# A six-layer cross network on one core: part of the transposes of input and output moved from TensorE to transposing DMAs

**Chip, cores, metric.** One Trainium2 chip (trn2), one NeuronCore. The metric is device time in microseconds (us), the median of the executions of a kernel; all executions told of here are of the fast state, none more than 1.5% above the fastest of its kernel. A span, read from a profile, runs from the first to the last instruction of one execution and is some 1.8 us shorter than that execution's time.

## The reference

```python
B, F, D, L = 1024, 26, 32, 6
Din = 832                      # min(F*D, 1024): six chunks of 128 columns and a ragged one of 64
# x0: (1024, 832), ws: (6, 832, 832), bs: (6, 832), all bfloat16
def reference(x0, ws, bs):
    x = x0
    for l in range(6):
        x = x0 * (x @ ws[l] + bs[l]) + x
    return x
```

## The kernel before

The layers work on the transposed activations: features on the partitions, the 1024 rows of the batch in the free dimension. So x0 has to be turned once at the start, and the result once at the end. Both are done on TensorE by matmuls against an identity, with an eviction from PSUM by ScalarE or VectorE in turn.

```python
# loads, all issued by SyncE in this order (shortened)
add_dma("sp", bs_nat[:, :], bs[:, :], ...)
for h in range(2):                      # x0 in two halves of 512 rows, 832 KB each
    add_dma("sp", xnat[:, h*4:(h+1)*4, :], x0[h*512:(h+1)*512, :], ...)
add_w_tail(0)                           # the last 64 rows of ws[0], twice
for dc in range(7):                     # ws[0] by columns of 128, 192 KB each
    add_dma("sp", w_sb[:, 0, 0:6, dc*128:...], ws[0, 0:768, dc*128:...], ...)
    if dc == 1:
        plan.op("sp", lambda e: None, reads=[("xnat", ...all...)], record=False)  # wait for x0
# ... ws[1] to ws[5], whole ...

# TensorE: 40 warm-up matmuls on the identity, the biases, then
for h in range(2):
    for kc in range(6):                 # 4 transposes into one PSUM bank, one eviction
        for i2 in range(4):
            pe_mm(bank, ..., xnat[:, bt, kc*P:(kc+1)*P], ident, ...)
        evac_copy(consumer, x0T[:, kc, hcols(h)], ps[bank], ...)
# ... the ragged chunk ("fold"): two halves of the batch packed on 128 partitions ...

# each layer: 3 groups of 2 chunks x 2 halves (28 matmuls of 128x512 each), then a fold group (14)
# per job: ScalarE adds the bias out of PSUM into tbuf, VectorE multiplies by x0T, then adds x
for l in range(6):
    pending_T = []
    for gi, dcs in enumerate(dc_groups):
        emit_group(l, dcs)
        if last:                        # output transposes one group late, and a store per pair
            if pending_T:
                emit_out_transposes(pending_T.pop(0))
            pending_T.append(dcs)
    emit_fold_group(l, 0)
    # last layer: the rest of the pending transposes, then those of the fold and its store
```

## Time and profile before

| | before |
|---|---|
| time, median of 5 (later of 15) | 138.91 us |
| span of the profiled execution (its own time: 139.71 us) | 137.9 us |
| layer 0 begins on TensorE | 10.43 us |
| group 2 of the last layer done | 125.6 us |
| last eviction done | 133.1 us |

The program is a chain of three stretches, and a gain in one is read from that stretch: up to layer 0 (loads and input transposes), from there to the end of the last layer's group 2 (TensorE alone), and from there to the end (VectorE, then a store). The prediction below shows the lines. In them PE is TensorE, PEld its weight loads, ACT ScalarE, DVE VectorE, POOL GpSimd, and SPq SyncE's queue of DMA issues; `out<-in` are the tiles written and read, xN is how many instructions a line takes together, and `[0.19 <-ACT tbuf L488]` says that the engine stood idle for 0.19 us, until that instruction released it.

### The profile page before, as it was taken

How to read it: one execution, taken by the hardware profiler on the slowest of the kernel's cores; microseconds unless marked ns; L12 is line 12 of the kernel's file. 1: busy time of each engine (PE TensorE's matmuls, PEld its weight loads, DVE VectorE, ACT ScalarE, POOL GpSimd, SP SyncE). 2: the span in 40 equal slices, each digit the busy share in tenths (PEclk: the TensorE clock that was granted, in tenths of full speed). 3: DMA queues.
4: the chain of work that ended last, by engine and by line, in shares of the span. 5: the costliest groups of instructions: out<-in, count | busy, mean ns of one | idle time of the engine just before them, and what ended most of it. 6: DMA issues, size and time to landing. Idle time of an engine off the chain costs nothing.

```text
span 137.9 us, 1914 instructions
## 1 busy us (share of the span) xinstructions
PE 127.1 (92%) x748; PEld 57.2 (41%) x748; DVE 68.7 (50%) x169; ACT 60.7 (44%) x104; POOL 0.7 (1%) x6
## 2 busy tenths in 40 slices
PE   5969999999999999999999999999999999899600
PEld 5954343444334343434343443434343434345300
DVE  0072174574538290926553562917274726573950
ACT  4274336091706361542725172806336442725920
POOL 2000000000000000000000000000000000000000
PEclk9999999999999999999999999999999999999995
DMA  2998999999700000000000000000000000005075
GB/s 49 400 235 188 257 331 363 357 322 321 277 3 0 0 2 7 0 0 0 0 0 0 0 5 0 0 0 0 0 0 5 0 0 0 0 0 152 0 217 130
DMA packets 15604, 12.48 MB, mean 90 GB/s; under 512 B 6886, under 2 KB 15596, under 8 KB 15596
## 3 DMA queue, kind: packets, MB, share of 16 engines
q1 hardware_dynamic: 15596, 12.37, 29.7%
q8 instruction: 6, 0.10, 0.3%
q14 instruction: 2, 0.02, 0.0%
HBM read 10.66 MB, written 1.70 MB: 90 GB/s over the span
## 4 chain that ended last, share of the span: by engine, by line
PE 83%; DMA 5%; DVE 4%; ACT 2%; issue 1%; SPq 1%; DVEq 0%; ACTq 0%
PE ps L339 83%; DMA xnat<-in_x_dram 5%; ACT tbuf L488 2%; DVE xT L524 2%; DVE ybuf L509 1%; DVE xnat L359 1%; SPq L266 1%; DVEq L182 0%; ACTq L137 0%
## 5 line engine op out<-in xcount | busy, mean ns | idle before, releaser
L339 PE MATMUL ps<-xT,w_sb 128*128 128x512 bf16 (+3 forms) x490 | 96.9, 381 | 0.4 <-ACT tbuf L488 0.4
L488 ACT ACTIVATE tbuf<-ps,bias_sb 128x512 bf16<-128x512 f32 (+1 forms) x84 | 51.2, 687 | 65.5 <-PE ps L339 65.4
L339 PEld LDWEIGHTS ps<-xT,w_sb 128*128 128x128 bf16 (+3 forms) x490 | 39.3, 99 | 57.1 <-issue 15.1
L509 DVE TENSOR_TENSOR ybuf<-tbuf,x0T 128x512 bf16<-128x512 bf16 x78 | 32.8, 420 | 54.3 <-ACT tbuf L488 54.3
L524 DVE TENSOR_TENSOR xT<-ybuf,xT 128x512 bf16<-128x512 bf16 x65 | 27.6, 425 | 2.2
L339 PE MATMUL ps<-x0T,w_sb 128*128 128x512 bf16 (+3 forms) x98 | 19.3, 380 | 0.0
L339 PEld LDWEIGHTS ps<-x0T,w_sb 128*128 128x128 bf16 (+3 forms) x98 | 7.8, 99 | 11.3 <-issue 3.0
L359 DVE CAST x0T<-ps 128x512 bf16<-128x512 f32 x6 | 3.8, 684 | 7.4 <-PE ps L339 7.4
L524 DVE TENSOR_TENSOR xT<-ybuf,x0T 128x512 bf16<-128x512 bf16 x13 | 5.5, 425 | 0.4
L339 PE MATMUL ps<-ident 128*128 128x128 bf16 x40 | 4.1, 298 | 1.5 <-POOL ident L234 1.5
L339 PE MATMUL ps<-ident,xT 128*128 128x128 bf16 (+1 forms) x56 | 3.7, 216 | 1.7 <-DVE xT L524 0.9
L354 ACT ACTIVATE x0T<-ps 128x512 bf16<-128x512 f32 (+1 forms) x8 | 4.2, 596 | 0.9 <-PE ps L339 0.8
L339 PEld LDWEIGHTS ps<-ident 128*128 128x128 bf16 x40 | 3.9, 142 | 1.5 <-POOL ident L234 1.5
L339 PE MATMUL ps<-ident,xnat 128*128 128x128 bf16 (+1 forms) x56 | 3.4, 220 | 1.2 <-DMA xnat<-in_x_dram 1.2
L339 PEld LDWEIGHTS ps<-ident,xT 128*128 128x128 bf16 (+1 forms) x56 | 2.9, 97 | 3.1 <-DVE xT L524 1.1
L359 DVE CAST xnat<-ps 128x512 bf16<-128x512 f32 (+1 forms) x7 | 4.2, 643 | 0.0
L354 ACT ACTIVATE xnat<-ps 128x512 bf16<-128x512 f32 (+1 forms) x7 | 3.7, 578 | 0.6 <-PE ps L339 0.6
L339 PEld LDWEIGHTS ps<-ident,xnat 128*128 128x128 bf16 (+1 forms) x56 | 2.9, 99 | 1.5 <-DMA xnat<-in_x_dram 1.4
L410 ACT ACTIVATE bias_sb<-ps 128x36 f32<-128x36 f32 x1 | 0.2, 201 | 3.8 <-PE ps L339 3.8
L376 ACT ACT_TABLE_LOAD x1 | 1.3, 1283 | 0.7 <-PEq L774 0.7
L339 PE MATMUL ps<-ident,bs_nat 6*128 6x6 bf16 (+1 forms) x8 | 0.4, 169 | 0.0
L422 ACT ACTIVATE bias_sb<-ps 64x6 f32<-64x6 f32 x2 | 0.3, 172 | 0.1
(8 smaller groups left out, 1.4 us busy)
## 6 DMA issues: line engine op xcount, KB each, us to landing
w_sb<-in_ws_dram SPq DMA_DIRECT2D x5, 1248.0 KB, 11.7
xnat<-in_x_dram SPq DMA_DIRECT2D x2, 832.0 KB, 5.8
out_dram<-xnat SPq DMA_DIRECT2D x3, 512.0 KB, 3.7
w_sb<-in_ws_dram SPq DMA_DIRECT2D x12, 104.0 KB, 9.4
w_sb<-in_ws_dram SPq DMA_DIRECT2D x6, 192.0 KB, 4.9
out_dram<-xnat SPq DMA_DIRECT2D x1, 128.0 KB, 4.2
w_sb<-in_ws_dram SPq DMA_DIRECT2D x1, 96.0 KB, 3.7
bs_nat<-in_bs_dram SPq DMA_DIRECT2D x1, 9.8 KB
```

The lines of the kernel that those rows point to most:

```text
L266: return e.dma_start(out=out_ap, in_=in_ap).then_inc(sem, 16)
L339: return e.matmul(out_ap, lhsT=lhsT, rhs=rhs, start=start, stop=stop, tile_position=tile_position,)
L354: return e.activation(out=out_ap, in_=in_ap, func=ACTF.Copy)
L359: return e.tensor_copy(out=out_ap, in_=in_ap)
L376: lambda e: e.activation(out=act_scratch[:, :], in_=ident[:, 0:8], func=ACTF.Copy),
L410: lambda e: e.activation(out=bias_sb[:, 0:NKF, :], in_=ps[bank_][:, 0 : NKF * L], func=ACTF.Copy,),
L422: return lambda e: e.activation(out=bias_sb[hf * HP : hf * HP + R, F, :], in_=ps[bank][hf * HP : hf * HP + R, F * L : (F + 1) * L], func=A ...
L488: return e.activation(out=tbuf[p0:p1, tslot, :], in_=ps[bank][p0:p1, :], func=ACTF.Identity, bias=bias_sb[p0:p1, kc_slot, l : l + 1], scal ...
L509: return e.tensor_tensor(out=ybuf[p0:p1, yb, :], in0=tbuf[p0:p1, tslot, :], in1=x0_ap, op=ALU.mult,)
L524: return e.tensor_tensor(out=xout_ap, in0=ybuf[p0:p1, yb, :], in1=xin_ap, op=ALU.add,)
```

## The change

Its intent is to let the DMA engines, which are idle in the last layers, do part of the transposing. At the front, chunks 4 and 5 of x0 (`NPE = 4` stay on TensorE) come transposed straight from DRAM; at the end, chunks 0 to 3 of the result are transposed from SBUF to SBUF and stored in pairs. The loads are regrouped, SyncE's wait for x0 is dropped, and chunks 4, 5 and the ragged tail are stored as one.

```diff
+        NPE = 4
         for h in range(NH):
             add_dma("sp",
-                xnat[:, h * BT_PER_H : (h + 1) * BT_PER_H, :],
+                xnat[:, h * BT_PER_H : (h + 1) * BT_PER_H, 0 : NPE * P],
 ...
+        add_dma("sp", xnat[:, :, DF : DF + R], x0[:, DF : DF + R]...)      # ragged tail, 128 KB
 ...
             if l == 0:
-                add_w_tail(0)
                 for dc in range(NKC):
                     add_dma("sp", w_sb[:, 0, 0:NKF, c0 : c0 + cw], ...)
                     if dc == min(1, NKC - 1):
-                        plan.op("sp", lambda e: None, reads=[("xnat", ...)], record=False)
+                        for kc in range(NPE, NKF):
+                            add_dma_t("sp", x0T[:, kc, :], x0[:, kc * P : (kc + 1) * P], ...)
+                        add_w_tail(0)
 ...
-            for kc in range(NKF):
+                for kc in range(NPE):                                      # 40 transposes, not 56
 ...
+        def emit_out_dma_transposes(dcs):
+            for c in dcs:
+                plan.dma("sp", lambda e: e.dma_start_transpose(
+                    out=xnat[:, :, c * P : (c + 1) * P], in_=xfin[:, c, :]), ...)
+            emit_out_dma(dcs[0] * P, (dcs[-1] + 1) * P, list(dcs))
 ...
+            # last layer: all groups, DMA transposes of groups 0 and 1, the fold group,
+            # then TensorE's transposes of chunks 4, 5 and the fold, and one store of 640 KB
+                emit_out_dma(c0, D, list(tail_dcs) + ([F] if FOLD else []))
```

More of the change, by code (lines that the diff above doesn't have):

```diff
@@ L177, in bass_standalone__dcn_v2_cross__recsys_kernel @@
     NWARM = 40
+    DMA_T_OUT = True
+    DMA_T_IN = True
     NY = 2
@@ L270, in bass_standalone__dcn_v2_cross__recsys_kernel, with add_dma_t, emit @@
         add_dma("sp", bs_nat[:, :], bs[:, :], writes=[("bs_nat",)])
+        def add_dma_t(q, out_ap, in_ap, writes, reads=()):
+            sem = new_dma_sem()
+            def emit(e, out_ap=out_ap, in_ap=in_ap, sem=sem):
+                return e.dma_start_transpose(out=out_ap, in_=in_ap).then_inc(sem, 16)
+            plan.dma(q, emit, done=(sem, 16), reads=reads, writes=writes)
+        NPE = 4
         for h in range(NH):
-            bts = range(h * BT_PER_H, (h + 1) * BT_PER_H)
             add_dma(
                 "sp",
-                xnat[:, h * BT_PER_H : (h + 1) * BT_PER_H, :],
-                x0[h * NCOL : (h + 1) * NCOL, :].rearrange("(bt p) d -> p bt d", p=P),
-                writes=[("xnat", bt, kc) for bt in bts for kc in range(NKC)],
-            )
+                xnat[:, h * BT_PER_H : (h + 1) * BT_PER_H, 0 : NPE * P],
+                x0[h * NCOL : (h + 1) * NCOL, 0 : NPE * P].rearrange("(bt p) d -> p bt d", p=P),
+                writes=[("xnat", bt, kc) for bt in range(h * BT_PER_H, (h + 1) * BT_PER_H) for kc in range(NPE)],
+            )
+        add_dma(
+            "sp",
+            xnat[:, :, DF : DF + R],
+            x0[:, DF : DF + R].rearrange("(bt p) d -> p bt d", p=P),
+            writes=[("xnat", bt, F) for bt in range(BT)],
+        )
         def wkey(l, kc, dc, hf):
@@ L310, in bass_standalone__dcn_v2_cross__recsys_kernel @@
                     if dc == min(1, NKC - 1):
-                        plan.op(
+                        for kc in range(NPE, NKF):
+                            add_dma_t(
+                                "sp",
+                                x0T[:, kc, :],
+                                x0[:, kc * P : (kc + 1) * P],
+                                writes=[("x0T", kc, h2) for h2 in range(NH)],
+                            )
+                        add_w_tail(0)
+                        if False: plan.op(
                             "sp",
@@ L317, in bass_standalone__dcn_v2_cross__recsys_kernel @@
                                 for kc in range(NKC)
-                            ],
+                            ]
+                            + [("x0T", kc, h) for kc in range(NKF) for h in range(NH)],
                             record=False,
@@ L431, in bass_standalone__dcn_v2_cross__recsys_kernel @@
         for h in range(NH):
-            for kc in range(NKF):
-                bank = next_bank()
-                for i2 in range(BT_PER_H):
-                    bt = h * BT_PER_H + i2
-                    pe_mm(
-                        bank,
-                        ps[bank][:, i2 * P : (i2 + 1) * P],
-                        xnat[:, bt, kc * P : (kc + 1) * P],
-                        ident[:, :],
-                        True,
-                        True,
-                        reads=[("xnat", bt, kc), ("ident",)],
-                    )
-                consumer = "act" if cnt % 2 == 0 else "dve"
-                cnt += 1
-                evac_copy(
-                    consumer,
-                    x0T[:, kc, hcols(h)],
-                    ps[bank][:, :],
-                    bank,
-                    writes=[("x0T", kc, h)],
-                )
+            if True:
+                for kc in range(NPE):
+                    bank = next_bank()
+                    for i2 in range(BT_PER_H):
+                        bt = h * BT_PER_H + i2
+                        pe_mm(
+                            bank,
+                            ps[bank][:, i2 * P : (i2 + 1) * P],
+                            xnat[:, bt, kc * P : (kc + 1) * P],
+                            ident[:, :],
+                            True,
+                            True,
+                            reads=[("xnat", bt, kc), ("ident",)],
+                        )
+                    consumer = "act" if cnt % 2 == 0 else "dve"
+                    cnt += 1
+                    evac_copy(
+                        consumer,
+                        x0T[:, kc, hcols(h)],
+                        ps[bank][:, :],
+                        bank,
+                        writes=[("x0T", kc, h)],
+                    )
             if FOLD and h % 2 == 1:
@@ L679, in emit_out_transposes, with emit_out_transposes_fold @@
             emit_out_dma(dcs[0] * P, (dcs[-1] + 1) * P, list(dcs))
-        def emit_out_transposes_fold():
+        def emit_out_transposes_fold(store=True):
             assert BT_PER_H * R <= NCOL
@@ L712, in emit_out_transposes_fold, with emit @@
                     )
-            emit_out_dma(DF, DF + R, [F])
+            if store:
+                emit_out_dma(DF, DF + R, [F])
+        def emit_out_dma_transposes(dcs):
+            for c in dcs:
+                sem = new_dma_sem()
+                def emit(e, c=c, sem=sem):
+                    return e.dma_start_transpose(
+                        out=xnat[:, :, c * P : (c + 1) * P], in_=xfin[:, c, :]
+                    ).then_inc(sem, 16)
+                plan.dma(
+                    "sp",
+                    emit,
+                    done=(sem, 16),
+                    reads=[xkey(L, c, h) for h in range(NH)],
+                    writes=[("xnat", bt, c) for bt in range(BT)],
+                )
+            emit_out_dma(dcs[0] * P, (dcs[-1] + 1) * P, list(dcs))
         dc_groups = [list(range(i, min(i + 2, NKF))) for i in range(0, NKF, 2)]
@@ L717, in bass_standalone__dcn_v2_cross__recsys_kernel @@
             last = l == L - 1
-            pending_T = []
-            for gi, dcs in enumerate(dc_groups):
-                emit_group(l, dcs)
-                if last:
+            if not last:
+                for dcs in dc_groups:
+                    emit_group(l, dcs)
+                if FOLD:
+                    for g in range(NG):
+                        emit_fold_group(l, g)
+                continue
+            if DMA_T_OUT:
+                n_early = len(dc_groups) - 1 if FOLD else len(dc_groups) - 1
+                for gi, dcs in enumerate(dc_groups):
+                    emit_group(l, dcs)
+                for gi in range(max(n_early, 0)):
+                    emit_out_dma_transposes(dc_groups[gi])
+                tail_dcs = dc_groups[-1] if dc_groups else []
+                if FOLD:
+                    for g in range(NG):
+                        emit_fold_group(l, g)
+                for c in tail_dcs:
+                    for h in range(NH):
+                        bank = next_bank()
+                        for i2 in range(BT_PER_H):
+                            bt = h * BT_PER_H + i2
+                            pe_mm(
+                                bank,
+                                ps[bank][:, i2 * P : (i2 + 1) * P],
+                                xfin[:, c, bt * P : (bt + 1) * P],
+                                ident[:, :],
+                                True,
+                                True,
+                                reads=[xkey(L, c, h), ("ident",)],
+                            )
+                        consumer = "act" if tcnt[0] % 2 == 0 else "dve"
+                        tcnt[0] += 1
+                        evac_copy(
+                            consumer,
+                            xnat[:, h * BT_PER_H : (h + 1) * BT_PER_H, c * P : (c + 1) * P],
+                            ps[bank][:, 0 : BT_PER_H * P].rearrange(
+                                "p (bt d) -> p bt d", d=P
+                            ),
+                            bank,
+                            writes=[
+                                ("xnat", bt, c)
+                                for bt in range(h * BT_PER_H, (h + 1) * BT_PER_H)
+                            ],
+                        )
+                if FOLD:
+                    emit_out_transposes_fold(store=False)
+                c0 = tail_dcs[0] * P if tail_dcs else DF
+                emit_out_dma(c0, D, list(tail_dcs) + ([F] if FOLD else []))
+            else:
+                pending_T = []
+                for gi, dcs in enumerate(dc_groups):
+                    emit_group(l, dcs)
@@ L724, in bass_standalone__dcn_v2_cross__recsys_kernel @@
                     pending_T.append(dcs)
-            if FOLD:
-                for g in range(NG):
-                    emit_fold_group(l, g)
-                    if last and pending_T:
-                        emit_out_transposes(pending_T.pop(0))
-            if last:
+                if FOLD:
+                    for g in range(NG):
+                        emit_fold_group(l, g)
+                        if pending_T:
+                            emit_out_transposes(pending_T.pop(0))
                 while pending_T:
```

## The prediction

> **What bounds the kernel now.** I read the page's busy times first, then the chain that ended last, then the first 12 us and the last 20 us instruction by instruction, and last the DMA rates in stretches of 1 us.
>
> ```profile
> PE 127.1 (92%) x748; PEld 57.2 (41%) x748; DVE 68.7 (50%) x169; ACT 60.7 (44%) x104; POOL 0.7 (1%) x6
> DMA  2998999999700000000000000000000000005075
> PE 83%; DMA 5%; DVE 4%; ACT 2%; issue 1%; SPq 1%; DVEq 0%; ACTq 0%
> ```
>
> The reader is to see that TensorE is the bound, and that the DMA engines are idle from slice 12 to slice 35, so the weights are no limit once the layers run. What is not TensorE lies at both ends, and the instructions in order of time show it:
>
> ```profile
> 5.91 1.51 PE L339 MATMUL ps<-ident,xnat 128*128 128x128 bf16 x24
> 8.62 1.87 PE L339 MATMUL ps<-ident,xnat 128*128 128x128 bf16 x32 [1.21 <-DMA xnat<-in_x_dram]
> 10.43 19.29 PE L339 MATMUL ps<-x0T,w_sb 128*128 128x512 bf16 x98
> 29.65 88.59 PE L339 MATMUL ps<-xT,w_sb 128*128 128x512 bf16 x448
> 118.17 1.07 PE L339 MATMUL ps<-ident,xT 128*128 128x128 bf16 x16
> 120.54 5.25 PE L339 MATMUL ps<-xT,w_sb 128*128 128x512 bf16 x25 [0.19 <-ACT tbuf L488]
> 125.71 1.07 PE L339 MATMUL ps<-ident,xT 128*128 128x128 bf16 x16
> 126.71 2.03 PE L339 MATMUL ps<-xT,w_sb 128*64 128x512 bf16 x14
> ```
>
> Layer 0 begins at 10.43 us, after x0 was loaded in two halves and turned by 56 transposes on TensorE; the second half made TensorE wait until 8.62. From 10.43 to 118.17 it never pauses: layer 1 begins 19.22 us after layer 0. In the last layer 32 of 56 output transposes stand in front of or between the layer's own matmuls. After TensorE's main work the end is a chain of VectorE work and one store:
>
> ```profile
> 125.61 0.69 ACT tbuf L488
> 129.59 0.71 DVE xnat L359 x2
> 131.59 0.60 DVE xnat L359
> 132.78 0.33 DVE xnat L359
> ```
>
> The last full group of matmuls is done at 125.6, the last eviction at 133.1; the two last stores are issued at 132.87 and 133.34, and the program ends at 137.9. In the outside time there is 1.0 us more than in the span (138.91 against 137.9); I keep that offset.
>
> **What the Trainium skill says.** (1) "DMA: Bandwidth & Descriptors", section "DMA Transpose (X-bar)": the hardware reorders on the write side, into SBUF only, for 2-byte types, issued from SP or ACT, and transposes on one queue need no wait among them. The change keeps to all of it. (2) The same page, "Latency and other measured facts": 261 GB/s was measured for one transposing kernel, and about 350 to 400 for contiguous data. A 128x1024 bf16 chunk is 262,144 bytes, so an estimate from this page is 1.0 us of transfer. (3) "VectorE: DVE Perf Modes", section "The three transpose paths", gives 1309 ns for a 128x128 bf16 block by the DMA crossbar against 390 ns on TensorE. Taken eight times over for a chunk, that would be an estimate of 10.5 us. The two pages are a factor of ten apart for our size, and the trace of before has no DMA transpose that could decide; for TensorE the trace shows far less than that page's 390 ns in a row: 16 transposes in 1.07 us, 0.067 us each. (4) "DMA: Bandwidth & Descriptors", "Queues, rings and completion order": on each engine the descriptors are consumed in ring order. So what is issued first delays what is issued after it; the trace agrees, since the first half of x0 landed 4.7 us after its issue and the second, issued 0.45 us later, 6.9 us after.
>
> **The change at the front.** x0 is loaded as two pieces of columns 0 to 511 (512 KB each), then a 128 KB ragged tail, then the weight columns 0 and 1 of layer 0, then two DMA transposes straight from DRAM (chunks 4 and 5, 256 KB each), then the weight tails and the other columns. The wait of SyncE for x0 before the third weight column is gone. TensorE does 40 transposes in place of 56.
>
> ```profile
> 3.00:4.00 1.00, 1.00 (x12) 1.00 (x11) 0.00 (x0) 0.00 (x0) 0.00 (x0) 1.00 0.86 298
> 4.00:5.00 1.00, 1.00 (x12) 1.00 (x10) 0.00 (x0) 0.00 (x0) 0.00 (x0) 1.00 1.04 401
> 8.00:9.00 1.00, 0.38 (x7) 0.38 (x8) 0.45 (x1) 0.22 (x1) 0.00 (x0) 1.00 1.30 224
> ```
>
> The last number of these stretches is GB/s. Adding up the stretches, 0.37 MB have moved by 4.0 us, then 0.4 MB per us while x0 rows of 1664 B move, and 224 GB/s when the 256 B rows of weight columns do. In before the 1.70 MB of x0 are through at about 7.4 and release TensorE at 8.6, 1.2 us later. In after 1.05 MB are through at 5.7; the 0.13 MB tail at 224 GB/s at 6.3; the two columns (0.39 MB) at 8.05, landing at about 9.2. TensorE, which can begin at 5.97 as now (its warm-up ends then), needs 16, 16 and 8 transposes, about 2.5 us, and is ready at 8.5. So layer 0 begins at about 9.2, now bound by the weight columns: 1.2 us gained.
>
> The two transposes follow. At 224 GB/s, which I take because their source rows are 256 B as well, each occupies the queue 1.17 us; they land at 10.4 and 11.6. Chunk 4 is needed after 16 matmuls of 0.2125 us (12.6), chunk 5 at 13.5. Behind them are 0.21 MB of weight tails and columns 2 and 3: through at 13.1, landing at 14.3, needed 28 matmuls (5.95 us) after the start, at 15.2. So the slack is 0.9 us for both transposes together: more than about 1.6 us each and group 1 waits for its weights, more than about 2.1 us each and group 0 waits for its chunk.
>
> **The change at the end.** Chunks 0 to 3 of the result go by four DMA transposes from SBUF to SBUF, chunk pairs stored as before; chunks 4, 5 and the tail stay on TensorE, after the fold group, in one store of 640 KB. Group 2's last matmul now comes 115.2 us after layer 0 began (125.6 - 10.43). Its own work is five layers of 19.24, then 11.6 for two groups (to 118.17, counted from 106.6) and 5.8 for the third: 113.6. The difference, 1.6 us, is 16 transposes (1.07) and the pauses for banks next to them (0.5); it goes. With the start at 9.2, group 2 ends at 122.8; call it T.
>
> From T: ScalarE's first eviction 0.7, then four VectorE pairs of about 0.82 to T+4.0 (as at 126.3 to 129.6 now). Today two evictions of 0.64 come before the fold pair; now the fold pair follows at once (T+4.85), then two evictions of 0.65 and a small one of 0.41: T+6.6, where it takes 7.5 now. Meanwhile ScalarE does its three evictions to about T+5.8. The store is issued at T+6.8 = 129.6. Now the last store lands 4.2 us after issue and has 512 KB in front of it; the 640 KB at about 340 GB/s are 1.9 us, with 0.9 before the data and 1.4 after (both as in the last store now): 4.2, and 0.2 to the end. Span 134.0, time 135.0. Sum of gains: 1.2 at the start, 1.6 inside the last layer, 0.9 in the VectorE chain, 0.2 in the store, 3.9 of 137.9.
>
> Chunks 0 and 1 are ready near T-8 and T-7 and chunks 2 and 3 near T-2.5 and T-0.8. If a transpose takes up to about 3 us from issue to landing, the second pair is in SBUF at about T+4, its store is out of the way by T+7, and nothing shows. I add 0.3 us for what I have not seen: 135.3.
>
> **The rivals.** A: as above, hidden. For it: page (2), idle DMA engines in the last layers. B: the transposes move data at a third of that, 3 to 4 us of queue each. At the end that still nearly hides; at the front it doesn't: at 3.3 us each the two take 4.3 us more than 2 times 1.17, of which 0.9 is slack, and the start's gain is gone: about 3.4 us lost, time about 138.5. The narrow place is thus the front, not the end. C: page (3) holds, 10 us each. Layer 0 then waits until about 30 us for chunk 5 (about 15 us lost), and at the end four in a row from T-8 last 42 us, some 25 us beyond the present end: 165 to 180 us. D: with SyncE's wait gone, weights crowd x0. Against it: they are behind x0 in the same ring, so at most tenths of a us.
>
> **Range and chances.** I give A about 0.5, B 0.2 with a spread from 136 to 142, C or something between B and C 0.3. A gives 134 to 136; two per cent faster is 136.1, so A is on the near side with 1 us to spare. That makes 0.5 faster, 0.2 within 2%, 0.3 slower. The range runs from A at its best, 133.6, to 150, and leaves out only the worse part of C.
>
> **What would show it.** In the profile after: layer 0's first matmul near 9.2 us, with the wait before it ended by weight columns; no pause of TensorE at chunks 4 and 5 or before group 1 (a wait on x0T by a DMA of over 0.5 us there is B or C); time from issue to landing of the transposes near 2 to 3 us; from group 2's end to the last eviction 6.6 us; no store of chunks 2 and 3 in flight when the last is issued. I am wrong if the transposes take over 2 us of queue each, or if issuing one keeps SyncE for several us.

## The result, and the profile after

The changed kernel takes 134.29 us (8 runs, 133.93 to 134.5) against 138.91 (15 runs). The ratio is 0.966, with a 95% interval of 0.9647 to 0.9674. Here and below a ratio is the mean time of one kernel's runs over that of the other's of the same rounds, so not quite the ratio of the medians quoted.

TensorE's instructions in order of time in the kernel after, at the front (start, duration, what; an idle time before stands in brackets, and there is none after the first row):

```profile
1.51 4.45 PE L363 MATMUL ps<-ident 128*128 128x128 bf16 x40 [1.51 <-POOL ident L236]
5.89 0.46 PE L363 MATMUL ps<-ident,bs_nat 6*128 6x6 bf16 x8
6.29 2.79 PE L363 MATMUL ps<-ident,xnat 128*128 128x128 bf16 x40
9.01 19.29 PE L363 MATMUL ps<-x0T,w_sb 128*128 128x512 bf16 x98
```

Layer 0 begins at 9.01 us in place of 10.43, and from its first instruction to the end of the last layer's matmuls at 124.4 TensorE no longer waits for anything: not for x0, not for the two transposed chunks, not for weights. (A start read from one trace is good to some tenths: the same 40 warm-up matmuls took 4.10 us in the trace before, 4.45 here and 3.66 in that of end_only below.) In the chain that ended last TensorE is now one piece from there:

```profile
1.51 120.97 PE ps L363 x660
122.48 0.69 ACT tbuf L513
...
128.45 0.33 DVE xnat L383
```

Group 2 of the last layer ends at 122.48, so 113.47 us after layer 0 began; the last eviction ends at 128.78, 6.3 us later; the span is 132.7. What the DMAs took, from the table of issues (count, KB, us from issue to landing), is this:

```profile
out_dram<-xnat SPq DMA_DIRECT2D x2, 512.0 KB, 3.1
out_dram<-xnat SPq DMA_DIRECT2D x1, 640.0 KB, 3.4
...
xnat<-xT SPq DMA_TRANSPOSE x4, 3.2
x0T<-in_x_dram SPq DMA_TRANSPOSE x2, 4.5
```

A transpose from SBUF to SBUF lands 3.2 us after its issue, one from DRAM at the busy front 4.5. The SyncE instructions of the end show how long issuing keeps SyncE, and that the work is done in time:

```profile
113.31 2.82 SPq L746 DMA_TRANSPOSE xnat<-xT  x2
118.07 0.39 SPq L663 DMA_DIRECT2D out_dram<-xnat  x1
119.12 2.85 SPq L746 DMA_TRANSPOSE xnat<-xT  x2
123.85 5.39 SPq L663 DMA_DIRECT2D out_dram<-xnat  x2
```

Two transposes take 2.8 us to issue, a store 0.39. The second pair is stored from 123.85 on and is out of the way 2 us before the last store is issued at 128.87.

### The profile page after: what moved, and what is told of

The parts are those of the page before. It is cut to its first block, busy times and chain, and to the rows that moved or that the text cites.

```text
span 132.7 us, 1811 instructions
## 1 busy us (share of the span) xinstructions
PE 124.7 (94%) x700; PEld 55.2 (42%) x700; DVE 65.0 (49%) x163; ACT 57.7 (44%) x98; POOL 0.7 (1%) x6
## 4 chain that ended last, share of the span: by engine, by line
PE 91%; DVE 4%; ACT 1%; issue 0%; DVEq 0%; POOLq 0%; POOL 0%
PE ps L363 91%; DVE ybuf L534 1%; DVE xT L549 1%; DVE xnat L383 1%; ACT tbuf L513 1%; DVEq L184 0%; POOLq L184 0%; POOL ident L233 0%; POOLq L236 0%; POOLq L866 0%
## 5 line engine op out<-in xcount | busy, mean ns | idle before, releaser
L383 DVE CAST x0T<-ps 128x512 bf16<-128x512 f32 x4 | 2.5, 684 | 7.4 <-PE ps L363 7.4
L378 ACT ACTIVATE x0T<-ps 128x512 bf16<-128x512 f32 (+1 forms) x6 | 3.3, 596 | 0.1
L363 PE MATMUL ps<-ident,xT 128*128 128x128 bf16 (+1 forms) x24 | 1.9, 212 | 1.4 <-DVE xT L549 1.4
L363 PE MATMUL ps<-ident,xnat 128*128 128x128 bf16 (+1 forms) x40 | 2.8, 243 | 0.0
L363 PEld LDWEIGHTS ps<-ident,xT 128*128 128x128 bf16 (+1 forms) x24 | 1.1, 96 | 2.3 <-DVE xT L549 2.3
L378 ACT ACTIVATE xnat<-ps 128x512 bf16<-128x512 f32 (+1 forms) x3 | 1.5, 524 | 0.4 <-PE ps L363 0.4
L383 DVE CAST xnat<-ps 128x512 bf16<-128x512 f32 (+1 forms) x3 | 1.6, 595 | 0.0
```

The costliest lines, as they stand in the source:

```text
L363: return e.matmul(out_ap, lhsT=lhsT, rhs=rhs, start=start, stop=stop, tile_position=tile_position,)
L378: return e.activation(out=out_ap, in_=in_ap, func=ACTF.Copy)
L383: return e.tensor_copy(out=out_ap, in_=in_ap)
```

## The experiments

Each is an edit of the kernel after or of the kernel before; ratios are against the kernel before.

### One end alone: front_only and end_only

front_only is the kernel after with `DMA_T_OUT = False` (the branch with the old end):

```diff
-    DMA_T_OUT = True
+    DMA_T_OUT = False
```

> The changed kernel with the old end (all 56 output transposes on TensorE). If the front's gain is what the two profiles show (layer 0 begins at 9.01 us in place of 10.43) and it passes undiminished to the end, 1.4 us of the 4.6 belong to it: about 137.5 us, layer 0 beginning near 9.0. A rival, that the whole gain is made at the end and an earlier front is eaten by something later, expects 138.9.

end_only is the kernel before with the last layer's code of the kernel after:

```diff
+            if DMA_T_OUT:   # the last layer of the kernel after, word for word
+                ... emit_out_dma_transposes(groups 0 and 1); one store of chunks 4, 5 and tail
```

> The old front with the changed end (four DMA transposes, merged last store). If the parts add up: 138.9 less 3.2, about 135.7 us, layer 0 beginning at 10.4, group 2's end near 123.9, last store landing about 3.4 us after its issue. If the end's gain were only there with the early front, it would be above 136.5.

front_only: 137.75 us, ratio 0.9899 (0.9864 to 0.9935), layer 0 begins at 9.02. end_only: 135.76 us, ratio 0.975 (0.9721 to 0.9778), layer 0 begins at 10.54. The product 0.9899 x 0.975 is 0.965, the changed kernel's ratio 0.966: within the noise (front_only's interval is 0.5 us to either side) the two ends are independent, with about 1.4 us (0.0101 of 138.9) at the front and 3.5 us (0.025 of 138.9) at the end. The rivals of both expectations fall.

In front_only the pauses for banks are still there, in TensorE's instructions of the last layer:

```profile
116.54 1.07 PE L363 MATMUL ps<-ident,xT 128*128 128x128 bf16 x16
117.75 0.39 PE L363 MATMUL ps<-xT,w_sb 128*128 128x512 bf16 x1
118.33 0.39 PE L363 MATMUL ps<-xT,w_sb 128*128 128x512 bf16 x1 [0.19 <-ACT tbuf L513]
118.91 5.25 PE L363 MATMUL ps<-xT,w_sb 128*128 128x512 bf16 x25 [0.19 <-ACT tbuf L513]
```

After 16 transposes (1.07 us) single matmuls wait for ScalarE's evictions; with the DMA transposes neither the transposes nor the waits are in the trace. One rival was not run: the transposes of chunks 0 to 3 left on TensorE, but placed after all of the layer's matmuls. What a new order alone would give of the 3.5 us is thus not shown.

### What of the front's gain is the DMA transpose's: pe_in and no_wait

```diff
-        NPE = 4
+        NPE = 6     # pe_in: the kernel after, all six chunks of x0 on TensorE
```

> The changed kernel, but all six chunks of x0 go by TensorE: columns 0 to 767 are loaded in two halves, no DMA transpose at the front, still no wait of SyncE. My theory, that the front gains because fewer bytes of x0 stand before TensorE's transposes and there are 16 fewer of them, expects layer 0 near 10.2 and 135.5 us. The rival, that the gain comes from the dropped wait and the new order of the loads and not from the DMA transposes, expects 134.3 us.

pe_in: 135.13 us, ratio 0.9704 (0.9675 to 0.9733); layer 0 begins at 9.78. That lies between end_only (0.975) and the kernel after (0.966), so both sides were half right: regrouping the loads without any DMA transpose gives 0.0046 of 138.9, 0.6 us, and the transposes of chunks 4 and 5 the other 0.0044, also 0.6 us. Each of these ratios has an interval of 0.2 to 0.4 us to either side, so the split is good to some tenths. TensorE's front in pe_in:

```profile
5.99 1.51 PE L363 MATMUL ps<-ident,xnat 128*128 128x128 bf16 x24
7.75 1.87 PE L363 MATMUL ps<-ident,xnat 128*128 128x128 bf16 x32 [0.25 <-DMA xnat<-in_x_dram]
9.78 2.56 PE L363 MATMUL ps<-x0T,w_sb 128*128 128x512 bf16 x11 [0.16 <-ACT x0T L378]
```

The second half of x0 releases TensorE at 7.75, where it did at 8.62 in the kernel before and at 8.51 in end_only, which has the same end as pe_in. To see whether the dropped wait is the cause, no_wait drops that alone in the kernel before:

```diff
-                    if dc == min(1, NKC - 1):
-                        plan.op("sp", lambda e: None, reads=[("xnat", bt, kc) ...], record=False)
```

> The kernel before, with only SyncE's wait for x0 dropped. pe_in has shown that 0.6 us of the front's gain needs no DMA transpose. If the wait was what cost it, layer 0 begins near 9.8 us and the time is 0.6 less, ratio about 0.995. My prediction (rival D there) said that the wait matters by tenths at most: then the ratio is 1.000 within 0.002, and the 0.6 us come from the ragged tail and the weight tails moved behind.

no_wait: 139.03 us, ratio 1.0007 (0.9995 to 1.0019). The wait is worth nothing. So, by elimination, the 0.6 us come from the rest of the regrouping: the ragged tail apart from the halves, and the weight tails moved back. At the 0.4 MB per us of the front the 0.13 MB of tail that no longer comes with the halves would be 0.33 us (an estimate). The trace of pe_in shows more: the second half landed at 7.71 and the tail at 8.30 (issued at 1.67 and 2.20), so TensorE starts on the half 0.6 us before all of x0 is there. What the moved weight tails add was not separated.

### Is the front the narrow place: dup_in and npe2

dup_in issues each front transpose twice, the second time into a scratch tile:

```diff
                             add_dma_t("sp", x0T[:, kc, :], x0[:, kc * P : (kc + 1) * P], ...)
+                            add_dma_t("sp", xdup[:, kc - NPE, :], x0[:, kc * P : (kc + 1) * P], ...)
```

> The changed kernel with each of the two front transposes issued twice, the second time into a scratch tile that nobody reads (the output stays right). That adds 2.8 us of issue and of queue ahead of the weight tails and columns. If the slack at the front is between 0.2 and 0.9 us as I worked out, TensorE pauses 1.9 to 2.6 us in layer 0 before group 1 and the time is 136.2 to 136.9. If there is slack of 3 us or more, 134.3 as without.

dup_in: 136.95 us, ratio 0.9856 (0.9812 to 0.99). That is 2.66 us over the kernel after (136.95 - 134.29), a shade above the expected band: nearly all of the 2.8 us that I had counted for the two more transposes shows. TensorE's instructions in layer 0:

```profile
8.20 4.77 PE L370 MATMUL ps<-x0T,w_sb 128*128 128x512 bf16 x20
13.87 1.04 PE L370 MATMUL ps<-x0T,w_sb 128*128 128x512 bf16 x4 [0.91 <-DMA x0T<-in_x_dram]
15.58 0.95 PE L370 MATMUL ps<-x0T,w_sb 64*128 64x512 bf16 x4 [0.67 <-DMA w_sb<-in_ws_dram]
17.08 0.60 PE L370 MATMUL ps<-x0T,w_sb 128*128 128x512 bf16 x2 [0.55 <-DMA w_sb<-in_ws_dram]
17.85 13.03 PE L370 MATMUL ps<-x0T,w_sb 128*128 128x512 bf16 x68 [0.16 <-DMA w_sb<-in_ws_dram]
```

First chunk 5 comes late, then the weight tails, then the weight columns of group 1. The instructions that write the weights, in the stretch that holds columns 2 and 3, give their landing; first the kernel after (issue from 9.9 to 10.6 us, then us from issue to landing):

```profile
L268 SPq DMA_DIRECT2D w_sb<-in_ws_dram x2: 541/566/592, 9.9 to 10.6; - x2
DMA to landing us min/median/max: 4.2/4.2/4.2
```

Column 2 was issued at 9.93 and landed at 14.2, column 3 at 10.57 and 14.8. Group 1 begins at 14.84 with two matmuls on column 2; its third is the first that reads column 3:

```profile
15.28 0.38 PE L363 MATMUL ps<-x0T,w_sb 128*128 128x512 bf16 x1
```

The slack that the prediction put at 0.9 us is thus about 0.5 for column 3 in this trace, and 0.7 for column 2. In dup_in, the same for column 3 alone:

```profile
L269 SPq DMA_DIRECT2D w_sb<-in_ws_dram x1: 540/540/540, 14.5 to 14.5; - x1
DMA to landing us min/median/max: 3.3/3.3/3.3
```

It was issued at 14.53, 4.0 us later (the last of the four transposes kept SyncE 2.25 us), but landed sooner after it, at 17.8. The matmul that reads it first begins the last row of TensorE's instructions above, at 17.85, 2.6 us later than in the kernel after: the 3.0 us by which the column landed later, less the slack of 0.5. That agrees with the 2.66 us of the times.

npe2 moves two more chunks of x0 to DMA transposes:

```diff
-        NPE = 4
+        NPE = 2
```

> The changed kernel with chunks 2 to 5 of x0 by DMA transpose in place of 4 and 5. My theory says that the front is the narrow place: SyncE issues a transpose in 1.4 us and each stays in the queue about as long, so two more of them push weight columns 2 and 3 back by 2.8 us beyond a slack of under 0.9. TensorE then waits in layer 0 for x0T and for weights, and the time is about 136.5. The rival, that transposes by DMA are cheap and more of them are better, expects layer 0 to begin near 8.3 us without a pause, and 133.7.

npe2: 136.17 us (134.77 to 136.68), ratio 0.978 (0.9722 to 0.9838), near the 136.5 expected. (By the 2% rule this one is unclear against the kernel before; against the kernel after, 0.9647 to 0.9674, the intervals don't touch.) The profiled execution was the one of 134.77, and its trace is not that of the others, which took 136.15 and more. It shows layer 0 beginning at 7.00 and then pausing twice for transposed chunks (0.38 and 0.52 us); where the other executions lose some 1.4 us more, no trace shows. Enough is measured to say that four transposes at the front are worse than two.

### The other end's limit: all_out

```diff
-                n_early = len(dc_groups) - 1 if FOLD else len(dc_groups) - 1
+                n_early = len(dc_groups)
-                tail_dcs = dc_groups[-1] if dc_groups else []
+                tail_dcs = []
```

> The changed kernel with chunks 4 and 5 of the result by DMA transpose too, stored as a pair, and the tail on its own. A transpose from SBUF takes 1.3 us to issue and 3.2 us to land; the last one is issued near 126.5 and lands at 129.7, only then is its pair stored, where TensorE's path is ready at 128.8. My theory expects about 0.8 us more than the changed kernel, 135.1. The rival, that taking the last work from TensorE and from the evictions helps here as it does for chunks 0 to 3, expects 134.0 or less.

all_out: 135.27 us, ratio 0.973 (0.9704 to 0.9756), 1.0 us above the kernel after and near the 135.1 expected. The stores of the end in its SyncE instructions:

```profile
124.51 2.85 SPq L746 DMA_TRANSPOSE xnat<-xT  x2
129.21 1.00 SPq L663 DMA_DIRECT2D out_dram<-xnat  x2
```

The last pair is ready to be stored at 129.21, although TensorE and the evictions are done at 127.8 in this trace. For work that nothing follows, the DMA's 3.2 us from issue to landing are on the path; on TensorE half a chunk takes 0.40 us for its four transposes and 0.6 to 0.7 for its eviction.

### What the last store is worth: merge_store and before_again

merge_store makes the last two stores of the kernel before into one:

```diff
+        def emit_out_transposes(dcs, store=True):
 ...
-                        emit_out_transposes(pending_T.pop(0))
+                        emit_out_transposes(pending_T.pop(0), store=False)   # the last pair
 ...
-            emit_out_dma(DF, DF + R, [F])
+            emit_out_dma(DF - 2 * P, DF + R, [F - 2, F - 1, F])
```

> The kernel before, with only its last two stores (512 KB and 128 KB) made one of 640 KB after the last eviction. My prediction put the gain of the store at 0.2 us; the profiles show 0.9 less from the last eviction to the end. If the merging makes that difference, about 138.0 us; if it was something else (the store of chunks 2 and 3 being out of the way, or chance in the one profile of before), 138.7 or more.

merge_store: 138.91 us, ratio 0.9975 (0.9946 to 1.0004). By the point value the merging is worth some 0.3 us, and nothing is not excluded. The 0.9 us by which the store's part differed between the first two profiles needed another explanation, so the kernel before was run unchanged for a second trace.

> The kernel before, unchanged, for a second trace. In the first trace the last two stores took 3.7 and 4.2 us to land, where the same stores took 3.1 and 3.4 in front_only, and its span was 137.9 where unprofiled runs had 137.1. If that was chance of one execution, this trace has stores of 3.1 to 3.4 us and a span near 137.1; if it belongs to the kernel, 3.7 to 4.2 us and 137.9 again. The time is that of before, 138.9 to 139.2.

before_again: 138.95 us, ratio 1.0005 (0.9991 to 1.0018), and a span of 137.0. Its stores:

```profile
out_dram<-xnat SPq DMA_DIRECT2D x3, 512.0 KB, 3.1
...
out_dram<-xnat SPq DMA_DIRECT2D x1, 128.0 KB, 3.4
```

In the first trace these rows read 3.7 and 4.2. Its last stores were late by chance: that execution's span of 137.9 is 0.8 above the 137.1 or so of unprofiled ones. From the last eviction to the end it is 4.1 us in the second trace and 3.8 in that of merge_store, which agrees with the 0.3 us of its ratio.

### Versions beyond the change: nwarm32, split_store, both

```diff
-    NWARM = 40
+    NWARM = 32
```

> The changed kernel with 32 warm-up matmuls in place of 40. In the trace after, TensorE never pauses from 1.51 us on: the 40 warm-up matmuls (4.45 us) now stand on the path to layer 0, while the first half of x0 has landed about 0.9 us before they end and weight column 1 about 0.4 us before layer 0 begins. My theory expects layer 0 to begin about 0.35 us earlier, held by weight column 1, and 133.9 us. If the front is held by loads as my prediction said, nothing changes: 134.3.

nwarm32: 133.74 us, ratio 0.9618 (0.9594 to 0.9642), 0.6 us below the kernel after. Its front:

```profile
1.52 3.53 PE L363 MATMUL ps<-ident 128*128 128x128 bf16 x32 [1.52 <-POOL ident L236]
...
8.52 18.98 PE L363 MATMUL ps<-x0T,w_sb 128*128 128x512 bf16 x95 [0.17 <-DMA w_sb<-in_ws_dram]
```

The warm-up was on the path after the change. With it shorter, TensorE waits in layer 0 for weight column 1 (issued at 3.86, landed at 8.48), the bound that the prediction had named.

split_store cuts the last store:

```diff
+        def emit_out_dma(c0, c1, chunk_keys, bts=None):                  # bts: rows to store
 ...
-                emit_out_dma(c0, D, list(tail_dcs) + ([F] if FOLD else []))
+                emit_out_dma(c0, DF, list(tail_dcs), range(0, BT_PER_H))     # rows of the first half
+                emit_out_dma(c0, DF, list(tail_dcs), range(BT_PER_H, BT))    # of the second
+                emit_out_dma(DF, D, [F])                                     # ragged tail
```

> The changed kernel with its last store of 640 KB cut in three: chunks 4 and 5 of the first half of the rows as soon as they are evicted (about 1.1 us before the rest), of the second half, and the ragged tail. If the end after the last eviction is set by the bytes that are left (640 KB took 1.9 us to move), 0.4 to 0.6 us are gained: 133.8. If two more issues on SyncE and the small rows of the tail eat it, 134.3.

split_store: 133.69 us, ratio 0.9613 (0.9589 to 0.9637), 0.6 us below the kernel after, as expected.

> The two together. If they are independent, as they stand at the two ends: 133.4 us, ratio to the kernel before about 0.960.

both: 133.29 us (133.03 to 134.51), ratio 0.9583 (0.9559 to 0.9608), the fastest of all and close to the sum of the two gains (134.29 less 0.55 and 0.60 is 133.1). The profiled execution was the slowest, 134.51 us, and shows why: in layer 0 TensorE stands for 1.09 us in group 1, before weight column 3.

```profile
8.88 6.00 PE L363 MATMUL ps<-x0T,w_sb 128*128 128x512 bf16 x28 [0.43 <-DMA w_sb<-in_ws_dram]
15.97 13.03 PE L363 MATMUL ps<-x0T,w_sb 128*128 128x512 bf16 x67 [1.09 <-DMA w_sb<-in_ws_dram]
```

Column 3 was issued at 10.76 and landed at 15.93, 1.2 us later than in the kernel after, while group 1 began only 0.3 us earlier (14.50 against 14.84). Why it landed late the trace does not tell, and the five faster executions (133.03 to 133.44) have no trace.

## Why the prediction was right, point by point

The time was said to be 135.3 with gains of 3.9 us in the span; it is 134.29, inside the range and faster by more than 2% as the chances leaned. The range, up to 150, was wide, so the terms say more than it does.

- **Rival A, B or C.** A holds: the transposes are hidden. A chunk's transpose keeps SyncE 1.24 to 1.44 us; from SBUF its data move for about 1.25 us at 190 to 230 GB/s, where the prediction took 224 GB/s and 1.17 us for one from DRAM. Rival C (10 us) is refuted by 3.2 and 4.5 us to landing; B (3 to 4 us of queue) by the 1.25 us, and at the front by the 1.4 us between the landings of the two (10.4 and 11.8). The prediction was right to give rival D, the dropped wait, no weight, as no_wait shows.
- **The start of layer 0.** Predicted 9.2, found 9.01. The reason given was not the one that bound, so that the number is near is in part luck: weight column 1 was to be last, at 9.2, but it landed near 8.6 (issued at 3.74, 4.9 us), while TensorE, said to be ready at 8.5, was ready only at 9.01. It never paused, and the path ran through its own warm-up, biases and 40 transposes. The column was first read by the third matmul, at 9.46, so it had 0.8 us to spare; in nwarm32, with TensorE earlier, TensorE waits for it.
- **The two chunks at the front.** Said to land at 10.4 and 11.6; issued at 5.79 and 7.28 and landing 4.6 and 4.5 us later, they were there at 10.4 and 11.8, 1.5 to 2 us before TensorE came to them (16 and 20 matmuls of 0.2125 us after 9.01: 12.4 and 13.3).
- **The slack behind them.** Said to be 0.9 us, found to be 0.5. The place was right, the size too kind: column 3 landed at 14.8 in place of 14.3, and was needed at 15.3, where 15.2 was said. (The working took the start of group 1 for both columns, and 28 matmuls for 5.95 us; they took 5.83.) Two things the sum had wrong or left out: from 9 to 14 us the DMA engines were busy but moved 140 to 232 GB/s, 190 on average, where 224 was counted; and behind the two transposes SyncE comes to the weight tails only at 8.66 us. They were not separated.
- **The last layer.** Predicted 113.6 us from layer 0 to the end of group 2, found 113.47, against 115.17 before.
- **The chain after it.** Predicted 6.6, found 6.3, against 7.5; the fold pair follows the four pairs at once, as worked out, and the three evictions take 1.5 us in place of 1.7.
- **The store and the offset.** These two were both off, and that they cancel is luck. The trace of before had stores late by 0.8 us and an execution of 139.71; the prediction set its span beside the median 138.91 and so took an offset of 1.0, where it is 1.8 (134.47 against 132.7 in the profiled run after). And from the last eviction to the end it counted 4.6 us, 4.2 of them for the store, where 3.9 were found, 3.4 of them for the store. So the offset made the forecast 0.8 us too short and the end 0.7 too long; what is left of the miss is 0.6 us in start, layer and chain, all of them found shorter, and the 0.3 that was added for the unseen. Against the second trace of before (10.24, then 115.17 to the end of group 2, 7.5 to the last eviction, 4.1 to the end) the gains are 1.2, 1.7, 1.2 and 0.2: 4.3 of the 4.6 that the medians show, the rest within the spread of single executions.

## What to carry to other kernels

In these runs a transposing DMA is worth its while where its latency has work beside it: in the middle of the last layer it frees TensorE and the evicting engines, while for the very last chunks TensorE's way is shorter. At a loaded front it is one more transfer in the queue, and what it costs is read from what stands behind it, not from its own landing. When one bound goes, look at what was free before: here the warm-up matmuls had come onto the path. And before a term is read off one trace, set that execution's own time beside the median.

## What the Trainium skill lacked or had wrong

- "VectorE: DVE Perf Modes", section "The three transpose paths", gives 1309 ns for one 128x128 block by the DMA crossbar and, below its table, about 90% of DMA bandwidth for that crossbar, which the prediction overlooked when it set this page against the other; it doesn't say which of the two holds for several blocks in one DMA. Eight blocks in one DMA of 128x1024 took 3.2 us from issue to landing from SBUF to SBUF, and 4.5 us from DRAM beside other loads: far from eight times 1309 ns.
- "DMA: Bandwidth & Descriptors", section "Latency and other measured facts", gives 261 GB/s and 350 to 400 GB/s for transposing DMAs. At this size, with nothing else in the queue, the trace after shows 190 to 230 GB/s, in packets of under 512 B.
- That page's "DMA Transpose (X-bar)" names no issue time, and none stands elsewhere on the page for a transpose of this size on this chip: 1.24 to 1.44 us of SyncE each, against 0.39 for a plain store of 512 KB. Whether this issue time or the queue set the limit at the front was not separated.
